# Six groups of two chunks in a chunked delta rule: chunk groups regrouped and w_in fetched earlier

## The chip, the cores and the metric

The kernel runs on one core of a Trainium2 chip. The metric is the device time of one execution in microseconds (us). The core has TensorE (PE in the profile, with its weight loads as PEld), VectorE (DVE), ScalarE (ACT), GpSimd (POOL) and SyncE (SP). Here SP issues every DMA, in program order.

## The reference

Two stages follow each other. The first is a delta-rule recurrence over 768 tokens, for 4 batch entries and 8 heads of 48 dimensions; k is divided by its norm:

```python
for t in range(S):
    kt, vt, bt = (k_n[:, :, t], v[:, :, t], beta[:, :, t, None])
    y[:, :, t] = np.einsum('bhd,bhde->bhe', q[:, :, t], state)
    v_old = np.einsum('bhde,bhd->bhe', state, kt)
    state = state + bt[:, :, :, None] * np.einsum('bhd,bhe->bhde', kt, vt - v_old)
```

The second takes the 3072 tokens' 384 values (8 heads of 48) through a wide layer of 1024:

```python
h = x @ w_in
e = np.exp(h - np.max(h, axis=-1, keepdims=True))
solu = h * e / (np.sum(e, axis=-1, keepdims=True) + 1e-09)
ln = (solu - mean(solu)) / np.sqrt(var(solu) + 1e-06) * g_ln
return ln @ w_out
```

## The kernel before

**Units.** The sequence is cut into 12 chunks of 64 tokens. A *unit* is one chunk of one pair of batch entries, so 128 rows; there are 24, u0 to u23, in the order chunk 0 pair 0, chunk 0 pair 1, chunk 1 pair 0 and so on. Names end in chunk and pair: `h_3_0` is h of u6, whose chunk is 3.

**Delta rule of a unit.** Inside a chunk the recurrence becomes a triangular system. `gram` multiplies K by K and K by Q per head on PE; ACT copies the first (`g`) to SBUF and SP sends it to DRAM (`gd`); DVE masks the second (`pm`). `chain` then applies the state: products `kps` and `yps`, r = v - kps on DVE, `ups` with the inverse, `u` on ACT, `cps` and the rest of `yps`, the state `st` updated on DVE, and the result split into two fp16 parts `xh` (ACT) and `xl` (DVE), which SP transposes by DMA (`xth`, `xtl`).

**Inversions of a group.** The triangular blocks of a *group* of chunks (the code's m) are inverted at once, one 32x32 block to a partition. `to_inv` gathers gd from DRAM into `ginv` (four DMAs with a full group); `norms` (DVE, first row `rst<-ginv`, last `nn`) makes norms and factors from its diagonal; `inv_begin` makes y with two DVE products, which a select on POOL makes triangular; `inv_step` runs 30 steps of two instructions each. For groups 0 and 1 a step's first ten columns are on DVE and the others on POOL; for later groups all is on POOL. `inv_end` copies the transpose on ACT (`ginv<-y`), sends y and the copy to DRAM (`zd`, `xd`) and gathers them back, laid out by unit (`zt`, `gx`, `gy`). `tlevel` joins the 32x32 blocks of a unit to 64x64 ones with small PE products (`mps`) and ACT copies into zt. The first of a group's chains needs this. Before, there are seven groups: chunk 0; chunks 1 and 2; 3 and 4; 5 and 6; 7 and 8; 9 and 10; chunk 11. In the groups of one chunk, half the partitions work on a copy of the other half.

**The wide layer of a unit.** `moe_h` makes h with 18 PE products of 512 columns (three fp16 passes over xl, xh and the two parts of w_in) in the one PSUM buffer for h; then the row maximum on DVE (`st<-h`, TENSOR_REDUCE), e on ACT, pr on DVE, the parts ph (ACT) and pl (DVE), two DMA transposes, and small row values, the rsqrt of them as a pow on POOL. `moe_out` has 24 PE products (`ops`), one DVE and one ACT instruction (`oc`) and the output DMA.

**Weights.** The weights come as 64-bit floats, whose bits `to_f32` reassembles: for each of 6 pieces of w_in a Square on ACT (`wc`), three DVE instructions and two POOL ones (`wf`), `win_hi` on ACT and `win_lo` on POOL; for each of 8 pieces of w_out the same with `wg`, `wout_hi` and, on DVE, `wout_lo`.

**What sets the order.** The kernel is recorded first. Each part is a stream with a time from a table at the end of the kernel function (in units of chunk steps; u0's chain is 0); that time is the priority of what it records. `Recorder.order` runs a list scheduler with a cost model over the record and so writes one fixed order for each engine, and there each instruction waits for all ahead of it. Every recorded instruction is issued from one line, L265, so the profile has one line for all, and the tile names tell them apart. The table puts a group's begin `tn` 5.4 steps before its end of preparation `e`, w_in's loads at -11.5 and -11.0 and group 1's gather at -10.8.

Of the kernel before, what the change touches and what calls it, by code (L numbers as in the profile page):

```python
# [8 lines left out]
F32 = mybir.dt.float32  # L9
# [10 lines left out]
NB = 7  # L20
# [280 lines left out]
def chunks_of(m):  # L301
    return [ch for ch in (2 * m - 1, 2 * m) if 0 <= ch < NC]
# [3 lines left out]
def kernel(  # L306
# [86 lines left out]
    def load_w_in(k, q, t0, t1):  # L393
        yield t0
        f = slice(512 * q, 512 * q + 512)
        raw = p3.tile([P, 512], w_in.dtype, tag="pr", name=f"wi_{k}_{q}")
        sp.dma_start(kb=512, out=raw, in_=w_in[k, q])
        yield t1
        w = p2.tile([P, 512], F32, tag="wf", name=f"wf_{k}_{q}")
        to_f32(w, raw, SC, 512, f"i{k}{q}")  # L400
        act.copy(out=win_hi[:, k, f], in_=w)
        gps.tensor_tensor(out=win_lo[:, k, f], in0=w, in1=win_hi[:, k, f], op=ALU.subtract)
# [95 lines left out]
    def gram(m, u, t0):  # L498
# [31 lines left out]
    last0 = [None]  # L530

    def to_inv(m):
        gi = p2.tile([P, 32, 32], F32, tag="ginv", name=f"ginv_{m}")
        ginv[m] = gi
        for b in range(4):
            blk = b % 2
            for z in range(1 if len(units(m)) == 4 else 2):
                src = gdt[m].rearrange("t u h j -> t (u h) j")
                n = H * len(units(m))
                ls = slice(0, n)  # L540
                sp.dma_start(
                    kb=128, out=gi[32 * b + 16 * z : 32 * b + 16 * z + n],
                    in_=src[32 * b : 32 * b + 32, ls, blk * 32 : blk * 32 + 32].rearrange("j l i -> l j i"),
                )
# [32 lines left out]
    def inv_end(m):  # L577
# [11 lines left out]
        n = 16 * len(chunks_of(m))  # L589
        src = gdt[m].rearrange("t u h j -> t (u h) j")  # L590
        for b in range(4):
            blk = b % 2
            r0 = 32 * b
            rows = slice(r0, r0 + 32)
            sp.dma_start(kb=128, out=zz[rows, 0:n, blk * 32 : blk * 32 + 32], in_=zd[r0 : r0 + n].rearrange("l j i -> j l i"))
            if blk == 0:
                for t, r1 in ((xx, r0), (xy, r0 + 32)):
                    sp.dma_start(kb=128, out=t[r1 : r1 + 32, 0:n], in_=xd[r0 : r0 + n].rearrange("l j i -> j l i"))
            else:
                sp.dma_start(kb=128, out=xx[rows, 0:n], in_=src[rows, 0:n, 0:32])  # L600
# [224 lines left out]
    for i in range(6):  # L825
        add(load_w_in(i // 2, i % 2, -11.5 if i < 2 else -11.0, -8 + 0.1 * i))
# [4 lines left out]

    for m in range(1, NB):
        f = 4 * m - 2
        nu = len(units(m))
        e = f if m > 1 else f - 2.5
        for u in range(nu):
            tg = e - 9 + 0.9 * u if m > 1 else -11.2 + 0.05 * u
            ch, bp = units(m)[u]
            add(once(tg - 0.9 if m > 1 else -11.8, lambda ch=ch, bp=bp: load_kq(ch, bp)))
            add(gram(m, u, tg))  # L840
            t = e - 1.9 + 0.9 * u
# [5 lines left out]
        add(inversion(m, tn + 0.6, e - 2.6 if m > 1 else -10))  # L847
# [35 lines left out]
def _lay(q, k, v, beta, moe_w_in, moe_w_out, moe_g_ln):  # L883
# [16 lines left out]
    bt = beta.reshape(2, 2, H, NC, 2, 32)  # L900
    bl = np.concatenate([bt[:, :, :, :1], bt, bt[:, :, :, -1:]], axis=3).reshape(2, 2, H, NB, 2, 2, 32)
# [27 lines left out]
```

## Time and profile before

| | before |
|---|---|
| time, median of 3 runs | 513.54 us (513.34 to 514.23) |
| time of the profiled execution | 512.04 us |
| its span | 510.2 us |
| busy PE / DVE / ACT / POOL | 368.2 / 318.6 / 192.9 / 294.0 us (72 / 62 / 38 / 58%) |
| DMA, mean of 16 engines | 70.8% for 72.21 MB |
| chain that ended last | POOL 28%, PE 22%, DVE 19%, issue 10%, DMA 9%, SP 7%, ACT 4% |

The page gives each engine's busy time, then the span in slices, then the chain of work that was followed back from the last instruction. The prediction also uses views of the trace. A row of a timeline has the start in us, the duration in us, the engine, the line, the operation, out<-in with shapes and, in brackets, the idle time ahead of it and what ended it. A row of the chain has start, duration, engine and out<-in; a group's row has the count, then busy us and mean ns. Rows of DMA issues have the count, KB each and us to landing.

### The profile page before, as it was taken

To read this page: it belongs to the slowest core of one execution; us is meant where nothing else is said; L and a number is where in the kernel's file an instruction comes from. 1 tells how busy PE (TensorE), PEld (TensorE's weight loads), DVE (VectorE), ACT (ScalarE), POOL (GpSimd) and SP (SyncE) were. 2 spreads that over 40 slices of the span, in tenths; PEclk is the share of its full clock that TensorE was granted. 3 is DMA by queue.
4 is the path that set the end of the run, shared out by engine and by line. 5 is a ranking of instruction groups with operands and counts; after the bars stand their busy time and mean duration, and the time that the engine had idled before them with its cause. 6 is when DMAs were issued, how large, how long until landed. Compare 5 with 4: busy or idle time off the path is not lost.

```text
span 510.2 us, 18246 instructions
## 1 busy us (share of the span) xinstructions
PE 368.2 (72%) x7744; PEld 233.9 (46%) x7744; DVE 318.6 (62%) x791; ACT 192.9 (38%) x382; POOL 294.0 (58%) x506
## 2 busy tenths in 40 slices
PE   3510070689579488997598997787969797899974
PEld 3410070455346345665366564444635464566532
DVE  3599999887884383655088664256597355455670
ACT  2210241465522143536144544224345345454450
POOL 3378385966558998984016886008989898100000
PEclk9999999877876699998799998898989899999998
DMA  8685662987989949977999587985656866744332
GB/s 212 159 255 98 155 169 65 161 171 174 172 162 165 179 113 160 168 135 161 189 165 144 145 162 151 160 162 95 107 118 144 145 114 128 131 64 99 73 68 61
DMA packets 180640, 72.21 MB, mean 142 GB/s; under 512 B 165520, under 2 KB 168976, under 8 KB 180560
## 3 DMA queue, kind: packets, MB, share of 16 engines
q1 hardware_dynamic: 180560, 71.06, 70.8%
q8 instruction: 60, 0.98, 0.9%
q14 instruction: 20, 0.16, 0.1%
HBM read 37.21 MB, written 16.52 MB: 105 GB/s over the span
## 4 chain that ended last, share of the span: by engine, by line
POOL 28%; PE 22%; DVE 19%; issue 10%; DMA 9%; SPq 7%; ACT 4%; POOLq 0%; DVEq 0%; ACTq 0%
POOL y L265 13%; POOL itmp L265 11%; PE h L265 7%; SPq L265 7%; PE ops L265 7%; DVE y L265 5%; DVE itmp L265 4%; DMA zt<-zd 3%; DMA ginv<-gd 3%; PE mps L265 2%; DVE wf L265 2%; DVE rst L265 1%; DVE st L265 1%; PE kps L265 1%; PE yps L265 1%
## 5 line engine op out<-in xcount | busy, mean ns | idle before, releaser
L265 POOL TENSOR_TENSOR y<-y,itmp 128x84 f32<-128x84 f32 (+16 forms) x190 | 100.7, 530 | 14.6
L265 POOL TENSOR_TENSOR itmp<-y,ginv 128x84 f32<-128x84 f32 (+16 forms) x190 | 93.3, 491 | 14.0
L265 DVE TENSOR_REDUCE st<-h 128x1 f32<-128x1024 f32 x24 | 29.3, 1222 | 87.5 <-PE h L265 82.2
L265 PE MATMUL qk<-kq 48*64 48x64 f32 x768 | 40.4, 269 | 24.9 <-DVE pm L265 15.6
L265 PE MATMUL gram<-kq 48*64 48x64 f32 x768 | 43.2, 270 | 18.8 <-DMA kq<-kq_dram 11.5
L265 POOL TENSOR_TENSOR st<-st,nhalf 128x1 f32<-128x1 f32 x24 | 13.2, 551 | 64.1 <-DVE st L265 64.1
L265 PEld LDWEIGHTS gram<-kq 48*64 48x64 f32 x768 | 37.5, 178 | 25.7 <-ACT g L265 6.3
L265 PEld LDWEIGHTS <-pth 128*128 128x128 f16 x384 | 37.6, 99 | 25.5 <-issue 1.7
L265 PE MATMUL h<-win_hi,xtl 128*128 128x512 f16 x144 | 45.4, 419 | 5.3 <-DVE pr L265 2.6
L265 PE MATMUL mps<-zt,gx 32*32 32x32 f32 x768 | 13.5, 205 | 48.6 <-issue 28.9
L265 PE MATMUL h<-win_lo,xth 128*128 128x512 f16 x144 | 46.7, 421 | 1.7 <-POOL win_lo L265 1.7
L265 PEld LDWEIGHTS qk<-kq 48*64 48x64 f32 x768 | 35.8, 178 | 25.3 <-DVE pm L265 16.1
L265 PEld LDWEIGHTS <-xth 128*128 128x128 f16 x288 | 28.4, 105 | 39.7 <-issue 14.8
L265 PE MATMUL ops<-wout_hi,ptl 128*128 128x384 f16 x192 | 38.7, 345 | 8.7 <-DMA ptl<-pl 6.8
L265 PE MATMUL h<-win_hi,xth 128*128 128x512 f16 x144 | 43.4, 411 | 0.0
L265 ACT ACTIVATE e<-h,st 128x1024 f32<-128x1024 f32 x24 | 26.7, 1114 | 38.0 <-DVE st L265 26.4
L265 POOL TENSOR_SCALAR_AFFINE_SELECT y<-y 128x1024 f32<-128x1024 f32 x7 | 9.4, 1346 | 53.5 <-DVE y L265 53.5
L265 DVE TENSOR_SCALAR st<-st 128x1 f32<-128x1 f32 (+1 forms) x216 | 35.5, 165 | 5.6
L265 PE MATMUL ops<-wout_lo,pth 128*128 128x384 f16 x192 | 36.9, 334 | 0.0
L265 PEld LDWEIGHTS mps<-zt,gx 32*32 32x32 f32 x768 | 10.1, 117 | 56.9 <-issue 34.8
L265 PE MATMUL ops<-wout_hi,pth 128*128 128x384 f16 x192 | 35.5, 326 | 0.0
L265 PE MATMUL cps<-u,kv 64*64 64x48 f32 x704 | 28.9, 235 | 9.1 <-ACT u L265 3.2
(94 smaller groups left out, 860.4 us busy)
## 6 DMA issues: line engine op xcount, KB each, us to landing
kq<-kq_dram SPq DMA_DIRECT2D x48, 192.0 KB, 4.5
kv<-kv_dram SPq DMA_DIRECT2D x24, 384.0 KB, 4.3
gd<-g SPq DMA_DIRECT2D x48, 128.0 KB, 3.3
out_dram<-oc SPq DMA_DIRECT2D x24, 192.0 KB, 2.2
zd<-y SPq DMA_DIRECT2D x7, 512.0 KB, 2.6
wi<-w_in_dram SPq DMA_DIRECT2D x6, 512.0 KB, 4.4
wo<-w_out_dram SPq DMA_DIRECT2D x8, 384.0 KB, 4.0
ginv<-gd SPq DMA_DIRECT2D x20, 128.0 KB, 4.2
```

Of the source, the lines that this page charges most:

```text
L265: fn(*[real(a) for a in args], **{k: real(a) for k, a in kw.items()})
```

## The change

There are six groups of two chunks each, so group m holds chunks 2m and 2m+1 and units 4m to 4m+3, and no group has copies. That moves all times of groups 2 and later by two steps (f = 4m), and group 2's begin lies 7 steps ahead, with its Gram products after u0's chain starts. Group 0 now has four units: four loads of kn for the norms, four Gram products, `tlevel` and `chain` with shifted priorities, and a shared tile (with tag "e") for g of its last two units. The gathers behind inversions 0 and 1 are cut in two halves of 16 blocks each. w_in's six pieces are loaded at -13.3, four of them into buffers of another pool (tag "kq"); the priority of their conversion stays at -8, so that it goes where the scheduler finds an engine idle. On the host, beta and kn are laid out for this.

```diff
-NB = 7
+NB = NC // 2
 def chunks_of(m):
-    return [ch for ch in (2 * m - 1, 2 * m) if 0 <= ch < NC]
+    return [2 * m, 2 * m + 1]
...
     def load_w_in(k, q, t0, t1):
-        raw = p3.tile([P, 512], w_in.dtype, tag="pr", name=f"wi_{k}_{q}")
+        raw = (p3 if k < 2 and q < 1 or k < 1 else p10).tile([P, 512], w_in.dtype, tag="pr" if k < 2 and q < 1 or k < 1 else "kq", name=f"wi_{k}_{q}")
...
     def load_kq(ch, bp):
-        if ch > 4:
+        if ch > 5:
             rec.after = raws[-1]
...
         act.activation(sq, k, AF.Square)
-        for v in (u, u + 2):
-            dve.tensor_reduce(out=xs[0][:, v], in_=sq, op=ALU.add, axis=AX.X)
+        dve.tensor_reduce(out=xs[0][:, u], in_=sq, op=ALU.add, axis=AX.X)
...
-        g = p2.tile([P, H, C], F32, tag="g", name=f"g_{ch}_{bp}")
+        if m or u < 2:
+            g = p2.tile([P, H, C], F32, tag="g", name=f"g_{ch}_{bp}")
+        else:
+            if u == 2:
+                ge[0] = p1.tile([P, 2, H, C], F32, tag="e", name="g_0")
+            g = ge[0][:, u - 2]
...
-        gps_ = ps_f.tile([P, H, C], F32, tag="fl", name=f"gram_{ch}_{bp}")
+        if m:
+            gps_ = ps_f.tile([P, H, C], F32, tag="fl", name=f"gram_{ch}_{bp}")
+        else:
+            gps_ = ps_ch.tile([P, H, C], F32, tag="ch", name=f"gram_{ch}_{bp}")
...
     def inv_end(m):
-        n = 16 * len(chunks_of(m))
-        for b in range(4):
-            sp.dma_start(kb=128, out=zz[rows, 0:n, blk * 32 : blk * 32 + 32], in_=zd[r0 : r0 + n].rearrange("l j i -> j l i"))
+        for l in (slice(0, 16), slice(16, 32)) if m < 2 else (slice(0, 32),):
+            n = l.stop - l.start
+            for b in range(4):
+                lanes = slice(r0 + l.start, r0 + l.stop)
+                sp.dma_start(kb=4 * n, out=zz[rows, l, blk * 32 : blk * 32 + 32], in_=zd[lanes].rearrange("l j i -> j l i"))
...
-    for bp in range(2):
-        add(once(-14 + .1 * bp, lambda bp=bp: load_kq(0, bp), lambda bp=bp: squares(bp)))
-        add(gram(0, bp, -13.5 + .01 * bp))
-        add(once(-9, lambda bp=bp: load_kv(0, bp), lambda bp=bp: fill_v(0, bp)))
-        add(tlevel(0, bp, -12.9 + 0.1 * bp, -12.85 + 0.1 * bp))
+    for u, (ch, bp) in enumerate(units(0)):
+        add(once(-14 + .1 * u, lambda ch=ch, bp=bp: load_kq(ch, bp)))
+        add(once(-13.7 + .01 * u, lambda u=u: squares(u)))
+        add(gram(0, u, -13.5 + .01 * u))
+        add(once(-9 + u, lambda ch=ch, bp=bp: load_kv(ch, bp)))
+        add(once(-9 + u, lambda u=u: fill_v(0, u)))
+        add(tlevel(0, u, -5 + u, -4.95 + u), -8)
...
-        add(load_w_in(i // 2, i % 2, -11.5 if i < 2 else -11.0, -8 + 0.1 * i))
+        add(load_w_in(i // 2, i % 2, -13.3 + 0.01 * i, -8 + 0.1 * i))
...
-        f = 4 * m - 2
-        e = f if m > 1 else f - 2.5
+        f = 4 * m
...
+            if m == 2:
+                tg = -2 + 0.9 * u
...
-        tn = e - 5.4 if m > 1 else -10.8
+        tn = f - 5.4 if m > 2 else f - 7 if m > 1 else -10.8
...
-        add(chain(m, u, i, i + 0.13, i + 0.25), -CH)
+        add(chain(m, u, i, i + 0.13, i + 0.25), -CH if m else -14)
```

Three places show how the written order moves. In its rows, numbers behind a name's chunk and pair are a buffer's; the shape is that of the output, and x2 or x4 says how many like it follow each other. The first is SP's queue around the gather of group 1 (`ginv_1<-gd_1`). Before:

```order
L265 DMA gd_1_390<-g_2_1_475 64x512 x2
L265 DMA kv_0_0_517<-kv_dram 128x768
L265 DMA kv_0_1_533<-kv_dram 128x768
L265 DMA ginv_1_553<-gd_1_390 32x32x32 x4
L265 DMA gx_1_586<-gd_1_390 32x32x32 x2
L265 DMA g_sb_602<-g_ln_dram 128x8
L265 DMA kq_3_0_604<-kq_dram 48x1024 x2
L265 DMA zd_0_623<-y_0_388 128x1024
```

After:

```order
L265 DMA zt_0_214<-zd_0_604 32x16x32
L265 DMA gd_1_541<-g_3_0_700 64x512 x2
L265 DMA gd_1_541<-g_3_1_755 64x512 x2
L265 DMA kv_1_0_829<-kv_dram 128x768
L265 DMA kv_1_1_886<-kv_dram 128x768
L265 DMA_TRANSPOSE xth_0_0_912<-xh_0_0_905 128x3x128
L265 DMA ginv_1_916<-gd_1_541 32x32x32
L265 DMA_TRANSPOSE xtl_0_0_953<-xl_0_0_910 128x3x128
L265 DMA ginv_1_916<-gd_1_541 32x32x32 x3
```

The gather of group 1 stood ahead of group 0's way back through DRAM (`zd_0`); it now stands behind that way back, behind two kv loads and among u0's two transposes.

The second is DVE around the row maximum of u0, `st_0_0<-h_0_0`. Before:

```order
L265 TENSOR_SCALAR wg_0_1182<-wo_0_960 128x384
L265 SCALAR_TENSOR_TENSOR wg_0_1182<-wo_0_960,wg_0_1182 128x384 x2
L265 TENSOR_SCALAR wg_1_1237<-wo_1_1021 128x384
L265 SCALAR_TENSOR_TENSOR wg_1_1237<-wo_1_1021,wg_1_1237 128x384 x2
L265 TENSOR_REDUCE st_0_0_1267<-h_0_0_1152 128x1
```

After:

```order
L265 TENSOR_TENSOR itmp_1_30_0_1605<-y_1_1179,ginv_1_916 128x10
L265 TENSOR_TENSOR y_1_1179<-y_1_1179,itmp_1_30_0_1605 128x10
L265 TENSOR_TENSOR pm_4_1_1608<-qk_4_1_1269,mask_93 128x512
L265 TENSOR_REDUCE st_0_0_1614<-h_0_0_996 128x1
L265 TENSOR_SCALAR st_0_0_1614<-st_0_0_1614 128x1
L265 SCALAR_TENSOR_TENSOR st_0_0_1614<-st_0_0_1614 128x1
L265 TENSOR_SCALAR st_0_0_1614<-st_0_0_1614 128x1 x4
L265 TENSOR_SCALAR wg_0_1661<-wo_0_1177 128x384
```

The row maximum of u0 stood behind two pieces of w_out; it now stands behind the last step of inversion 1, and w_out's first piece behind it.

The third is PE inside h of u6 (`h_3_0`) after the change, with group 2's first block products (`mps`, the second product of u8's blocks in the lower rows):

```order
L265 MATMUL mps0_2_0_3162<-zt_0_214,gx_2_2390 32x32 x16
L265 LDWEIGHTS xth_3_0_2777
L265 MATMUL h_3_0_3141<-win_lo_351,xth_3_0_2777 128x512
...
L265 MATMUL mps0_2_0_3162<-msb_2_0_3182,gx_2_2390 32x32 x2
L265 MATMUL mps32_2_0_3189<-msb_2_0_3182,gy_2_3065 32x32 x2
...
L265 MATMUL h_3_0_3141<-win_hi_344,xth_3_0_2777 128x512
```

In program order they stand apart only by weight loads and repeated rows of the same kind; h of u6 is thus finished behind these products, which need zt of group 2. On DVE the norms of group 3 stand behind u6's pr:

```order
L265 TENSOR_REDUCE st_3_0_3214<-h_3_0_3141 128x1
L265 TENSOR_SCALAR st_3_0_3214<-st_3_0_3214 128x1
L265 SCALAR_TENSOR_TENSOR st_3_0_3214<-st_3_0_3214 128x1
L265 TENSOR_SCALAR st_3_0_3214<-st_3_0_3214 128x1 x4
L265 SCALAR_TENSOR_TENSOR pr_3_0_3291,st_3_0_3214<-h_3_0_3141,e_3_0_3260 128x1024
L265 TENSOR_SCALAR rst_3_3336<-ginv_3_2954 128x32
```

Before the change, the norms of groups 3, 4, 5 and 6 stood behind the row maxima of u2, u7, u12 and u13.

More of the change, by code (lines that the diff above doesn't have):

```diff
@@ L529 @@
     ginv, yt = {}, {}
-    last0 = [None]
+    last0, ge = [None], [None]
     def to_inv(m):
@@ L534, in to_inv @@
         ginv[m] = gi
+        src = gdt[m].rearrange("t u h j -> t (u h) j")
         for b in range(4):
             blk = b % 2
[L537 to L544, printed above, removed]
+            r = slice(32 * b, 32 * b + 32)
+            sp.dma_start(kb=128, out=gi[r], in_=src[r, :, blk * 32 : blk * 32 + 32].rearrange("j l i -> l j i"))
     def inv_begin(m):
@@ L588, in inv_end @@
         xy = p1.tile([P, 4 * H, 32], F32, tag="gy", name=f"gy_{m}")
-        n = 16 * len(chunks_of(m))
         src = gdt[m].rearrange("t u h j -> t (u h) j")
-        for b in range(4):
-            blk = b % 2
-            r0 = 32 * b
-            rows = slice(r0, r0 + 32)
-            sp.dma_start(kb=128, out=zz[rows, 0:n, blk * 32 : blk * 32 + 32], in_=zd[r0 : r0 + n].rearrange("l j i -> j l i"))
[L596 to L600, printed above, removed]
+        for l in (slice(0, 16), slice(16, 32)) if m < 2 else (slice(0, 32),):
+            n = l.stop - l.start
+            for b in range(4):
+                blk = b % 2
+                r0 = 32 * b
+                rows = slice(r0, r0 + 32)
+                lanes = slice(r0 + l.start, r0 + l.stop)
+                sp.dma_start(kb=4 * n, out=zz[rows, l, blk * 32 : blk * 32 + 32], in_=zd[lanes].rearrange("l j i -> j l i"))
+                if blk == 0:
+                    for t, r1 in ((xx, r0), (xy, r0 + 32)):
+                        sp.dma_start(kb=4 * n, out=t[r1 : r1 + 32, l], in_=xd[lanes].rearrange("l j i -> j l i"))
+                else:
+                    sp.dma_start(kb=4 * n, out=xx[rows, l], in_=src[rows, l, 0:32])
         ztx[m], gxt[m] = zz, (xx, xy)
@@ L832 @@
     for m in range(1, NB):
-        f = 4 * m - 2
-        nu = len(units(m))
-        e = f if m > 1 else f - 2.5
-        for u in range(nu):
-            tg = e - 9 + 0.9 * u if m > 1 else -11.2 + 0.05 * u
-            ch, bp = units(m)[u]
+        f = 4 * m
+        for u, (ch, bp) in enumerate(units(m)):
+            tg = f - 9 + 0.9 * u if m > 1 else -11.2 + 0.05 * u
+            if m == 2:
+                tg = -2 + 0.9 * u
             add(once(tg - 0.9 if m > 1 else -11.8, lambda ch=ch, bp=bp: load_kq(ch, bp)))
             add(gram(m, u, tg))
-            t = e - 1.9 + 0.9 * u
+            t = f - 1.9 + 0.9 * u
             add(tlevel(m, u, t, t + 0.4))
@@ L844 @@
             add(once(f + u - 0.9, lambda m=m, u=u: fill_v(m, u)))
-        tn = e - 5.4 if m > 1 else -10.8
+        tn = f - 5.4 if m > 2 else f - 7 if m > 1 else -10.8
         add(begin(m, tn, tn + (0.5 if m > 1 else 0.01)))
-        add(inversion(m, tn + 0.6, e - 2.6 if m > 1 else -10))
+        add(inversion(m, tn + 0.6, f - 2.6 if m > 1 else -10))
     order = [(m, u) for m in range(NB) for u in range(len(units(m)))]
@@ L898, in _lay @@
     kq = con(np.stack([tr(k), tr(q)], axis=5))
-    bt = beta.reshape(2, 2, H, NC, 2, 32)
-    bl = np.concatenate([bt[:, :, :, :1], bt, bt[:, :, :, -1:]], axis=3).reshape(2, 2, H, NB, 2, 2, 32)
+    bl = beta.reshape(2, 2, H, NB, 2, 2, 32)
     bl = con(bl.transpose(1, 5, 4, 0, 2, 3, 6).reshape(P, NB, 32))
@@ L909, in _lay @@
     return {
-        "kn_dram": con(kn[0]),
+        "kn_dram": con(kn[:2].reshape(4, P, H, D)),
         "kv_dram": kv,
```

## The prediction

> **What bounds the kernel now.** I read the chain that ended last first, then the windows by stage, then the places where a unit's h is finished, then the rows of the chain between two inversions. A unit is one chunk of 64 tokens for one pair of batch entries; u0 to u23 are worked on in this order.
>
> ```profile
> POOL 28%; PE 22%; DVE 19%; issue 10%; DMA 9%; SPq 7%; ACT 4%; POOLq 0%; DVEq 0%; ACTq 0%
> ```
>
> No engine owns the chain. It goes over POOL while an inversion runs, and over DMA, SP, PE and DVE between two of them.
>
> ```profile
> core 0: us, PE busy (x) PEld busy (x) DVE busy (x) ACT busy (x) POOL busy (x), PEclk, DMA share, GB/s
> 108.00:204.00 96.00, 71.85 (x1601) 46.05 (x1595) 63.66 (x150) 38.12 (x79) 71.13 (x109) 0.80 0.88 165
> 204.00:448.00 244.00, 207.13 (x4567) 129.03 (x4565) 137.21 (x353) 105.28 (x214) 149.94 (x269) 0.94 0.76 143
> ```
>
> PE is at 85% in the long middle stage, so little is left there for a change that only removes idle time. In the stage ahead of it DVE, POOL and DMA are all at 66 to 88%, and no engine explains 96 us by itself.
>
> ```profile
> 107.96 1.22 DVE L265 TENSOR_REDUCE st<-h 128x1 f32<-128x1024 f32 x1 [0.39 <-PE h L265]
> 156.25 1.64 DVE L265 SCALAR_TENSOR_TENSOR pl<-pr,st,ph 128x1024 f16<-128x1024 f32 x1 [0.37 <-ACT ph L265]
> 204.19 1.22 DVE L265 TENSOR_REDUCE st<-h 128x1 f32<-128x1024 f32 x1 [5.41 <-PE h L265]
> 334.65 1.22 DVE L265 TENSOR_REDUCE st<-h 128x1 f32<-128x1024 f32 x1 [6.36 <-PE h L265]
> 430.44 1.22 DVE L265 TENSOR_REDUCE st<-h 128x1 f32<-128x1024 f32 x1 [4.42 <-PE h L265]
> 448.39 1.22 DVE L265 TENSOR_REDUCE st<-h 128x1 f32<-128x1024 f32 x1 [7.62 <-PE h L265]
> 490.42 1.23 DVE L265 TENSOR_REDUCE st<-h 128x1 f32<-128x1024 f32 x1 [1.89 <-PE h L265]
> ```
>
> The DVE timeline: each reduction is the row maximum that follows a finished h; here those of u0, u4, u12, u18, u19 and u23, and u2's pl. I call them R0, R4 and so on. From R0 to R4 a unit takes 24 us, from R4 to R23 15.1 us, from R18 to R23, with the last inversion over, 12.0 us. R23 to the end of the span is 19.8 us.
>
> ```profile
> 144.45 1.26 POOL L265 TENSOR_SCALAR_AFFINE_SELECT y<-y 128x1024 f32<-128x1024 f32 x1 [8.20 <-DVE y L265]
> 189.43 1.26 POOL L265 TENSOR_SCALAR_AFFINE_SELECT y<-y 128x1024 f32<-128x1024 f32 x1
> 270.88 1.26 POOL L265 TENSOR_SCALAR_AFFINE_SELECT y<-y 128x1024 f32<-128x1024 f32 x1 [4.95 <-DVE y L265]
> 344.46 1.26 POOL L265 TENSOR_SCALAR_AFFINE_SELECT y<-y 128x1024 f32<-128x1024 f32 x1 [29.61 <-DVE y L265]
> 389.93 1.26 POOL L265 TENSOR_SCALAR_AFFINE_SELECT y<-y 128x1024 f32<-128x1024 f32 x1
> 188.11 1.99 ACT L265 COPY ginv<-y 128x1024 f32<-128x1024 f32 x1
> 310.97 1.99 ACT L265 COPY ginv<-y 128x1024 f32<-128x1024 f32 x1 [6.59 <-POOL y L265]
> 431.36 1.96 ACT L265 COPY ginv<-y 128x1024 f32<-128x1024 f32 x1
> ```
>
> The POOL and ACT timelines: the select starts the POOL inversion of groups 2 to 6 (call the starts A2 to A6), the ACT copy behind it marks its end (E). Three of them give A to E: 43.7, 40.1 and 41.4 us; I take **41**. POOL then waits up to 29.6 us for the next group's y. So POOL isn't full: inversions alternate with a return path.
>
> ```profile
> 312.98 1.97 DMA xd<-ginv
> 320.36 4.27 DMA zt<-zd
> 324.67 0.45 PE mps L265 x30
> 337.76 0.19 DVE L265 TENSOR_SCALAR rst<-ginv 128x32 int32<-128x32 int32 x1 [1.69 <-DMA ginv<-gd]
> 341.90 1.23 DVE L265 TENSOR_TENSOR ginv<-ginv,nn 128x1024 f32<-128x1024 f32 x1
> ```
>
> The chain and DVE around it: E4 at 310.97, xd and the gathers into zt, group 4's first block product at 324.67 (13.7 after E4), the rest of u12's h, R12 at 334.65, group 5's norms from 337.76 (DVE has them behind R12), its two 1.23 us products, A5 at 344.46. The return path took 33.5 us.
>
> **The change part by part.** It takes one POOL inversion away (five become four) and gives group 0 four units instead of two. What is priced is when A2 comes and how long the ring of inversions and return paths runs from there.
>
> *The front.*
>
> ```profile
> 3.11 5.07 DMA kn<-kn_dram
> 25.06 1.47 DVE ginv L265
> 36.75 3.17 SPq L265 DMA_DIRECT2D ginv<-gd  x4
> 53.06 1.94 ACT L265 COPY ginv<-y 128x1024 f32<-128x1024 f32 x1 [19.80 <-issue]
> 57.54 1.22 DVE L265 TENSOR_TENSOR ginv<-ginv,nn 128x1024 f32<-128x1024 f32 x1
> 60.10 2.01 DVE wf L265 x2
> 72.30 0.49 ACT L265 ACTIVATE xh<-yps 128x384 f16<-128x384 f32 x1 [2.15 <-PE yps L265]
> 87.92 2.00 ACT L265 COPY ginv<-y 128x1024 f32<-128x1024 f32 x1 [11.74 <-DVE y L265]
> ```
>
> Now inversion 0 begins at 25.06 and ends at 53.06, u0's xh comes at 72.30, and inversion 1, whose gather was issued at 36.75, runs right behind inversion 0, 57.54 to 87.92. In the change the fourth kn is issued behind the first gd, and ACT copies the fourth g after its square: with the 5.07 us of a kn landing I add 2 us (0 if it lands unnoticed, 5 if all waits), and 1 us for w_in conversion ahead of the first step: inversion 0 ends near 56. The gathers into zt are now twice as many and stand behind one more gd, so for xh I take the 19.2 us of now plus 1.5: near 76.5. Only then can SP issue group 1's gather, since it stands behind u0's xth and xtl; now it stands ahead of everything of u0. Two transposes and four pieces at 0.8 us end near 82, and it lands near 86:
>
> ```profile
> gd<-g SPq DMA_DIRECT2D x48, 128.0 KB, 3.3
> ginv<-gd SPq DMA_DIRECT2D x20, 128.0 KB, 4.2
> zt<-zd SPq DMA_DIRECT2D x20, 128.0 KB, 4.2
> zt<-zd SPq DMA_DIRECT2D x8, 64.0 KB, 2.9
> L265 DVE SCALAR_TENSOR_TENSOR xl<-yps,xh 128x384 f16<-128x384 f32 x24 | 13.2, 549 | 0.1
> ```
>
> Norms are 4.1 us (337.76 to 341.90), the inversion 30.4 us as now, less the w_in pieces in it (the 2.01 us row and as much again), plus five chain instructions of about 0.55 us that DVE has between its steps. The order puts u0's reduction behind the last step, so **R0 is near 120**, 12 us later than now, though its h needs only xtl and w_in, ready by then. Bounds: 114 if the gather lands at 80, 126 if every piece waits as at its worst. The w_in conversions save nothing here: they end earlier, and R0 doesn't wait for them.
>
> The Trainium skill (DMA: Bandwidth & Descriptors, Rules for kernel authors) would have small transfers coalesced, since under 64 KB they are mostly overhead; here groups 0 and 1 are cut into halves. The rows say 2.9 us for a 64 KB piece against 4.2 for 128 KB, so a half does land sooner. By the rule alone the half would gain nothing and the sum would be 1.3 us higher.
>
> *R0 to A2.*
>
> ```profile
> L265 DVE SCALAR_TENSOR_TENSOR wg<-wo,wg 128x384 int32<-128x384 int32 x16 | 11.0, 689 | 0.4
> L265 DVE TENSOR_SCALAR wg<-wo 128x384 int32<-128x384 int32 x8 | 5.7, 715 | 1.8 <-DMA gd<-g 1.3 <-POOL win_lo L265 0.5
> L265 DVE TENSOR_TENSOR wout_lo<-wg,wout_hi 128x384 f16<-128x384 f32 x8 | 4.5, 575 | 3.5 <-ACT wout_hi L265 3.4
> ```
>
> Group 2's norms now stand ahead of u2's row maximum; in the change behind u2's pl. From R0 to the end of u2's pl it takes 49.9 us now. Less the norms and two products in it (6.6), plus two w_out slices that DVE has done before R0 now and does after it in the change (2 x (0.715 + 2 x 0.689), and one wout_lo, 0.575: 4.8), it is 48: norms near 168, and 6.6 us later **A2 near 174.7**, 30 us later than now. Bounds: 40 us if the stalls in that stretch go, 55 if the gather is late.
>
> *The ring.* Four inversions of 41 us are 164. Three return paths: PE's order has 15 of u6's 18 h products ahead of group 2's second block product, and DVE has group 3's norms behind u6's pr; groups 4 and 5 stand the same way behind R10 and R14. So E to block product 13.7, some 3 us of h and copies, 1.2 for the maximum, up to 4 for pr, 4.1 and 2.5 for norms and products: 28, 27 and 29 (group 5's gather stands behind four transposes of u13). Together 84; from below 75 with no wait for a gather, from above 3 x 33.5 = 100.5 as measured. E5 is then near 174.7 + 164 + 84 = 422.7. From E6 to R19 it is 17.0 us now; the change has u18's output product between group 5's block product and u19's h, so up to 24: I take 20, **R19 near 442.7**, against 448.39. Behind it the same units, 61.8 us to the end: 504.5. Lies beside other work: the smaller number of gathers, norms and POOL steps, and kv's scaling. The profiled run took 512.04 with a span of 510.2; the median is 513.54, 3.3 over the span. Forecast: **507.8, said as 508 us.**
>
> **The rivals.** *The cover rival, faster:* PE isn't held by the ring at all, because its block products come when zt is there. For it: DVE works only 63.66 of the 96 us from R0 to R4, and w_out is done on POOL ahead of A2, where now two slices are caught inside inversion 2. R4 at 190, 19 units at 14.5 us (between 12.0 and 15.1), 19.8 us: 485, a time of 488. Against it: the ring holds u5's exp behind E2 in ACT's order. *The late-ring rival, slower:* mechanism as forecast, but A2 comes at 177, every return path costs the measured 33.5, and R19 stands 24 behind E5: 177 + 164 + 100.5 + 24 + 61.8 = 527, a time of 531. With R19 24 behind E5 it loses to the kernel before from E5 later than about 424 (448.39 less 24). Rows speak for it: 33.5 is the one path measured whole. *It doesn't do what it says:* w_in early is of no use, and the inversion removed is one that lay beside other work; then R19 stays near 448.39 and the time at the median, 513.5.
>
> **How the numbers follow.** The forecast's ring (498 to 515) 0.42, the cover rival 0.22, the late ring 0.28, no effect 0.08. A measurement of this kernel tells 0.2%, about 1 us, from no change. Faster: 0.22 and 0.30 of the forecast's 0.42. Same: 0.04 of it, 0.04 of the last. Slower: 0.28, 0.08 and 0.04. So 0.52, 0.08, 0.40. The forecast's own range is 498 to 515; with both rivals, leaving a tenth out on each side, 484 to 528.
>
> **What would show it.** R0 near 120 with inversion 1's last DVE step right ahead of it; group 1's gather issued behind u0's transposes after 76; w_out done on POOL before A2 near 175; exactly four selects behind that, 67 to 72 us apart; PE waiting for zt inside u6's and u10's h; R19 some 20 us behind the last ACT ginv copy. It is wrong if selects follow each other closer than 60 us, if R0 comes before 108, or if PE waits for something else at the group borders.

## The result and the profile after

The changed kernel took 529.79 us in the median of 4 runs (528.26 to 532.73), the kernel before 513.44 us (512.15 to 514.23). The ratio is 1.0328, with a 95% interval of 1.0277 to 1.0378. It is slower, where 508 was forecast, and it lies outside the range, 1.8 us above its upper end. The profiled execution took 529.23 us, with a span of 527.5 us. Some kernels below had executions more than 1.5% over their fastest; the ratios leave these out, the medians do not.

First the page's busy line of the changed kernel, then its windows by stage, cut at the row maxima of u0 (R0), u4 (R4) and u19 (R19):

```profile
PE 382.6 (73%) x7744; PEld 243.9 (46%) x7744; DVE 306.7 (58%) x771; ACT 192.0 (36%) x382; POOL 258.6 (49%) x445
```

```profile
core 0: us, PE busy (x) PEld busy (x) DVE busy (x) ACT busy (x) POOL busy (x), PEclk, DMA share, GB/s
0.00:125.80 125.80, 54.12 (x1492) 43.47 (x1492) 84.79 (x204) 28.75 (x61) 73.10 (x123) 0.90 0.68 159
125.80:197.60 71.80, 59.99 (x1099) 36.16 (x1102) 53.81 (x129) 34.20 (x70) 39.92 (x52) 0.79 0.79 161
197.60:465.40 267.80, 217.53 (x4542) 135.22 (x4538) 135.59 (x354) 103.90 (x207) 141.83 (x261) 0.89 0.69 132
465.40:527.50 62.10, 50.94 (x632) 29.04 (x629) 32.52 (x87) 25.15 (x45) 3.72 (x10) 0.95 0.35 72
```

POOL lost 35 us of work and the kernel became slower. R0 came 17.8 us later than before (125.8 against 108.0), but R4 came 6.6 us earlier (197.6 against 204.2): what the front loses up to u0 it has regained by u4. The loss is all in the third row. From R4 to R19 the change took 267.8 us, the kernel before 244.2 (448.39 less 204.19): 23.6 more for the same fifteen units. The last stage is the same, 62.1 against 61.8.

That row also shows of what the 23.6 consist. PE is busy 217.5 us in it against 207.1 in nearly the same stretch before, with about as many products (4542 against 4567), at a granted clock of 0.89 against 0.94. So 10 us are the same work at a lower clock (0.89 x 217.5 and 0.94 x 207.1 are 194 and 195). The other 13 are time without work on PE (50.3 us against 36.9).

The POOL and ACT timelines of the changed kernel, put together in order of time, with the four selects that start the POOL inversions (A2 to A5) and the ACT copies that mark their ends (E2 to E5):

```profile
177.57 1.27 POOL L265 TENSOR_SCALAR_AFFINE_SELECT y<-y 128x1024 f32<-128x1024 f32 x1 [13.51 <-DVE y L265]
217.34 1.98 ACT L265 COPY ginv<-y 128x1024 f32<-128x1024 f32 x1 [3.16 <-POOL y L265]
247.36 2.25 POOL L265 TENSOR_SCALAR_AFFINE_SELECT y<-y 128x1024 f32<-128x1024 f32 x1 [21.62 <-DVE y L265]
287.46 1.96 ACT L265 COPY ginv<-y 128x1024 f32<-128x1024 f32 x1 [6.62 <-POOL y L265]
316.76 1.27 POOL L265 TENSOR_SCALAR_AFFINE_SELECT y<-y 128x1024 f32<-128x1024 f32 x1 [19.05 <-DVE st L265]
356.26 1.96 ACT L265 COPY ginv<-y 128x1024 f32<-128x1024 f32 x1 [4.81 <-POOL y L265]
391.92 1.27 POOL L265 TENSOR_SCALAR_AFFINE_SELECT y<-y 128x1024 f32<-128x1024 f32 x1 [14.64 <-DVE y L265]
433.52 1.99 ACT L265 COPY ginv<-y 128x1024 f32<-128x1024 f32 x1 [2.47 <-POOL y L265]
```

The inversions took 39.8, 40.1, 39.5 and 41.6 us, together 161.0. Between them lie three full return paths of 30.0, 29.3 and 35.7 us, together 95.0. From A2 to the last E it is 256.0 us, in the kernel before 286.9 (144.45 to 431.36, with five inversions). So the change did shorten this stretch, by 31 us: the inversions took 161.0 us in place of 207.5, but the three return paths 95.0 in place of 79.4 for four. Two of the four borders of the kernel before were nearly free: its A3 stood 1.3 us behind an E (189.43 against 188.11), since those norms were done early, and its A6 4.2 us (389.93 against 385.78). The other two took 40.4 (230.46 to 270.88) and 33.5 us. The two E of the kernel before that the prediction does not show (ACT timeline):

```profile
230.46 1.95 ACT L265 COPY ginv<-y 128x1024 f32<-128x1024 f32 x1 [5.71 <-POOL y L265]
385.78 1.97 ACT L265 COPY ginv<-y 128x1024 f32<-128x1024 f32 x1 [6.21 <-POOL y L265]
```

The 31 us were more than spent elsewhere: A2 came 33.1 us later, and from the last E to R19 it took 31.9 us against 17.0. That leaves R19 17.0 us later than before.

The last piece in detail. PE's timeline around the return of group 5, and six of the windows of 2 us there (columns as above):

```profile
438.80 0.23 PE L265 MATMUL yps<-st,kq 48*64 48x48 f32 x1 [2.92 <-DVE xl L265]
444.31 0.31 PE L265 MATMUL mps<-zt,gx 32*32 32x32 f32 x2 [2.31 <-DMA zt<-zd]
448.29 0.64 PE L265 MATMUL mps<-zt,gx 32*32 32x32 f32 x30 [3.67 <-DMA zt<-zd]
```

```profile
438.00:440.00 2.00, 1.20 (x62) 1.23 (x62) 0.56 (x2) 0.57 (x2) 0.00 (x0) 0.89 1.02 174
440.00:442.00 2.00, 2.00 (x9) 0.45 (x6) 0.55 (x1) 0.00 (x0) 0.00 (x0) 0.50 1.32 153
444.00:446.00 2.00, 0.31 (x2) 0.18 (x2) 1.43 (x3) 0.84 (x2) 0.00 (x0) 0.50 1.17 160
450.00:452.00 2.00, 2.00 (x7) 0.93 (x8) 0.72 (x2) 1.30 (x6) 1.12 (x3) 0.50 0.58 158
452.00:454.00 2.00, 2.00 (x41) 1.01 (x40) 0.00 (x0) 0.00 (x0) 0.33 (x2) 0.70 1.00 193
454.00:456.00 2.00, 2.00 (x72) 1.52 (x70) 0.00 (x0) 1.14 (x4) 0.00 (x0) 1.00 0.12 23
```

zt lands 14.8 us behind the last E, about as forecast (13.7). But then it takes 17.1 us to R19: in PE's order u17's output product, three units' block products and u20's and u21's first products stand ahead of u19's h, and for nearly the first 5 us of this the granted clock is 0.50. It had fallen behind the wait that ended at 438.80, and as PE went on waiting it did not rise until work came almost without a break. In the kernel before, only three of u19's h products were left when zt landed, and R19 came 1.2 us after that wait, with the clock at 1.00 from E6 on:

```profile
447.16 0.45 PE L265 MATMUL mps<-zt,gx 32*32 32x32 f32 x30 [2.40 <-DMA zt<-zd]
```

### The profile page after: what moved, and what is told of

Its sections match the earlier page's. It is cut to its first block, busy times and chain, and to the rows that moved or that the text cites. A ratio compares the mean times of both kernels' runs of the same rounds, so it can differ in the third digit from the quotient of the medians.

```text
span 527.5 us, 18160 instructions
## 1 busy us (share of the span) xinstructions
PE 382.6 (73%) x7744; PEld 243.9 (46%) x7744; DVE 306.7 (58%) x771; ACT 192.0 (36%) x382; POOL 258.6 (49%) x445
## 4 chain that ended last, share of the span: by engine, by line
POOL 30%; issue 19%; PE 15%; DVE 14%; SPq 9%; DMA 9%; ACT 4%; POOLq 0%; DVEq 0%; ACTq 0%
POOL y L265 13%; POOL itmp L265 12%; SPq L265 9%; PE h L265 5%; DVE y L265 4%; PE ops L265 4%; DVE itmp L265 4%; DMA kq<-kq_dram 3%; DMA zt<-zd 2%; POOL st L265 2%; PE ups L265 1%; PE mps L265 1%; DVE st L265 1%; DMA kn<-kn_dram 1%; DVE wg L265 1%
## 5 line engine op out<-in xcount | busy, mean ns | idle before, releaser
L265 POOL TENSOR_TENSOR y<-y,itmp 128x84 f32<-128x84 f32 (+16 forms) x160 | 80.0, 500 | 12.3
L265 POOL TENSOR_TENSOR itmp<-y,ginv 128x84 f32<-128x84 f32 (+16 forms) x160 | 76.6, 479 | 12.1
L265 DVE TENSOR_REDUCE st<-h 128x1 f32<-128x1024 f32 x24 | 29.3, 1223 | 88.4 <-PE h L265 79.6
L265 PE MATMUL gram<-kq 48*64 48x64 f32 x768 | 43.0, 270 | 34.1 <-DMA kq<-kq_dram 24.6
L265 PE MATMUL ops<-wout_hi,ptl 128*128 128x384 f16 x192 | 41.5, 364 | 7.4 <-DMA ptl<-pl 7.0
L265 PE MATMUL h<-win_hi,xth 128*128 128x512 f16 x144 | 45.2, 423 | 0.0
L265 PE MATMUL ups<-r,zt 64*64 64x48 f32 x704 | 29.4, 241 | 13.0 <-DVE r L265 13.0
L265 PE MATMUL ops<-wout_lo,pth 128*128 128x384 f16 x192 | 38.1, 342 | 0.0
L265 PE MATMUL yps<-st,kq 48*64 48x48 f32 x704 | 29.7, 240 | 11.3 <-DVE xl L265 10.5
L265 DVE SCALAR_TENSOR_TENSOR pl<-pr,st,ph 128x1024 f16<-128x1024 f32 x24 | 33.4, 1391 | 7.2 <-ACT ph L265 4.2
L265 ACT ACTIVATE ph<-pr,st 128x1024 f16<-128x1024 f32 x24 | 27.6, 1149 | 27.3 <-DVE pr L265 24.8
```

What stands on the lines that cost most here:

```text
L265: fn(*[real(a) for a in args], **{k: real(a) for k, a in kw.items()})
```

## The experiments

Each edit starts from the changed kernel unless it says otherwise; what isn't shown is unchanged. Ratios are to the kernel before, which ran on the same chip. It took 513.4 to 515.0 us on the chips used, so a difference between two times of the table can be off by 1.5 us; ratios are the safer comparison. From R4 to R19 the kernel before took 244.2 us.

| run | time, us | ratio (95% interval) | R4 to R19 in its profile, us |
|---|---|---|---|
| the change | 529.8 | 1.0328 (1.0277 to 1.0378) | 267.8 |
| short_inv | 510.3 | 0.9921 (0.9893 to 0.9949) | 249.0 |
| before_short | 500.4 | 0.9736 (0.9698 to 0.9773) | 233.3 |
| norms_1_earlier | 521.2 | 1.0128 (1.0103 to 1.0153) | 256.0 |
| norms_2_earlier | 517.1 | 1.0035 (1.0002 to 1.0067) | 245.5 |
| norms2_short | 496.4 | 0.9671 (0.9623 to 0.9720) | 225.5 |
| less_pe | 507.2 | 0.9877 (0.9844 to 0.9911) | 240.0 |
| w_in_late | 526.5 | 1.0223 (1.0181 to 1.0266) | 268.6 |
| before_w_in_early | 538.8 | 1.0502 (1.0454 to 1.0549) | 258.8 |
| gather_first | 530.1 | 1.0294 (1.0260 to 1.0328) | 266.2 |
| front_both | 517.8 | 1.0077 (1.0045 to 1.0109) | 257.4 |
| group2_early | 539.2 | 1.0467 (1.0427 to 1.0508) | 263.4 |
| kv_ahead | 521.9 | 1.0136 (1.0109 to 1.0163) | 259.1 |
| kv_only | 528.6 | 1.0278 (1.0233 to 1.0323) | 265.6 |
| keep_clock | 527.8 | 1.0232 (1.0174 to 1.0289) | |
| three_together | 516.1 | 0.9995 (0.9967 to 1.0023) | 243.2 |
| front_and_kv | 519.9 | 1.0089 (1.0056 to 1.0121) | 256.7 |
| front_kv_norms1 | 519.2 | 1.0077 (1.0044 to 1.0110) | 271.4 |
| norms2_kv_late_w_in | 509.9 | 0.9927 (0.9899 to 0.9954) | 241.9 |

### Is it the inversions?

**short_inv.**

```diff
+    def left_out(kw):
+        t = kw.get("in1")
+        for v in (kw.get("out"), t):
+            n = v.root.name.split("_") if isinstance(v, View) else [""]
+            if n[0] == "itmp" and int(n[1]) > 1 and 13 <= int(n[2]) <= 18:
+                return True
+        return False
...
     for o in ops:
         for fn, args, kw in o.calls:
+            if left_out(kw):
+                continue
```

> The changed kernel with steps 13 to 18 of the four POOL inversions (groups 2 to 5) left out, the order of everything else word for word the same; so its output is not the reference's. In the changed kernel's trace these six steps take POOL 8.5 us of each inversion. Ring theory (from A2 on, inversions and return paths alternate and every unit waits for them): the whole 4 x 8.5 = 34 us comes off, a time of 496 (up to 505 if PE takes over in places), and the return paths stay at 27 to 34 us. PE theory (the middle is slow because PE is at its limit under a lower clock, 0.89 against 0.94): POOL's work is hidden, at most 5 us come off, 525 to 530.

19.5 us came off, between the two. In its trace the inversions are together 27.1 us shorter (31.3, 31.6, 33.3 and 37.7), and the return paths 8.0 us longer (34.2, 33.3 and 35.5). Its window from R4 to R19:

```profile
200.50:449.50 249.00, 212.25 (x4546) 133.37 (x4546) 134.21 (x355) 103.87 (x207) 110.77 (x213) 0.88 0.73 142
```

So the inversions are on the path, but a return path is no fixed price. I read it so that it holds the units that stand between an E and the next norms, and these have a pace of their own: a shorter inversion leaves more of them to the return.

**before_short.** The same edit on the kernel before.

> The kernel before with steps 13 to 18 of its five POOL inversions (groups 2 to 6) left out, order unchanged; its output is not the reference's. This tests the premise that the kernel before is held by its inversions too: 5 x 8.5 = 42 us of POOL's work are gone. If inversions and return paths set the pace before as well, 20 us or more come off (493 or less). If the 16.3 us that a unit takes there from R4 to R19 are set by something else (PE's work and the waits inside a unit's own chain), 0 to 8 us come off: 506 to 514.

13.9 us of some 42 came off, a third, against 57% in the changed kernel (19.5 of 34). The premise of the forecast, that alternation sets the pace before as it does after, is only a third true. By this an inversion that is removed there is worth less than its length; no run removes a whole one.

**norms_1_earlier and norms_2_earlier.** With d = 1 and d = 2:

```diff
-            tg = f - 9 + 0.9 * u if m > 1 else -11.2 + 0.05 * u
+            tg = f - (9 + d) + 0.9 * u if m > 1 else -11.2 + 0.05 * u
...
-        tn = f - 5.4 if m > 2 else f - 7 if m > 1 else -10.8
+        tn = f - (5.4 + d) if m > 2 else f - 7 if m > 1 else -10.8
```

> The changed kernel with the Gram products and the norms of groups 3 to 5 put one step earlier in the table: the norms of group 3 stand behind u4's pr instead of u6's, those of group 4 behind u8's pl instead of u10's maximum, those of group 5 behind u13's maximum instead of u14's. Ring theory: the next inversion no longer waits for the group's own return path, so POOL starts it right behind the one before; A2 stays at 177, A3 follows E2 within 10 us instead of 28, and R19 comes 30 to 50 us before 465: 480 to 500. PE theory: selects come earlier, but PE is full; 525 to 530.

> The same, two steps earlier: norms of group 3 ahead of u4's maximum, of group 4 behind u8's pr, of group 5 behind u12's maximum. Ring theory: as one step earlier, with the return path gone from all three places, 475 to 495. PE theory: 525 to 530. A loss against one step earlier would mean that Gram products put earlier hold the units that are due.

8.6 and 12.7 us came off: the direction of the ring theory, far from its size. norms_2_earlier alone brings the kernel within 0.4% of the one before. In norms_2_earlier A3 comes at 220.97, ahead of E2 at 224.88 (POOL and ACT timelines):

```profile
220.97 1.27 POOL L265 TENSOR_SCALAR_AFFINE_SELECT y<-y 128x1024 f32<-128x1024 f32 x1
224.88 1.99 ACT L265 COPY ginv<-y 128x1024 f32<-128x1024 f32 x1 [0.60 <-POOL y L265]
292.07 2.25 POOL L265 TENSOR_SCALAR_AFFINE_SELECT y<-y 128x1024 f32<-128x1024 f32 x1 [17.43 <-DVE y L265]
360.78 1.27 POOL L265 TENSOR_SCALAR_AFFINE_SELECT y<-y 128x1024 f32<-128x1024 f32 x1 [18.49 <-DVE st L265]
```

One return path is gone, but A4 and A5 still follow 71 and 69 us behind, with POOL idle ahead of them: their norms now stand behind u8's pr and u12's maximum, and on the way to these PE waits for zt (3.3 us until 238.8, 6.2 until 295.3). Nor did all that the ring gained reach the units. The three return paths are 42.3 us shorter in sum and the last E comes 31.4 us earlier (402.15 against 433.52), but R4 comes 12.3 us later (209.9), and from the last E to R19 it takes 53.3 us instead of 31.9, so R19 comes only 10.0 us earlier. So once the norms are early, R19 no longer follows from the last E alone.

**norms2_short and less_pe.** Both take norms_2_earlier further: one with the six steps left out, the other with one pass of h left out of all units:

```diff
+    def left_out(kw):
+        v, r = kw.get("out"), kw.get("rhs")
+        return isinstance(v, View) and v.root.name.startswith("h_") and isinstance(r, View) and r.root.name == "win_lo"
...
+            if left_out(kw):
+                continue
```

> The changed kernel with norms two steps earlier (517.1) and steps 13 to 18 of the four POOL inversions left out (8.5 us each); its output is not the reference's. Neither PE's work (less by a third of h: 507.2) nor the inversions of the kernel before (13.9 of 42 us came off) account for the 16.4 us a unit takes there. If inversions still hold it, half or more of the 34 us come off: 500 or less. If the latency of a unit's own way (h, maximum, e, pr, transposes, with the POOL powers and PE's waits inside) holds it, at most 8: 509 to 517.

> The changed kernel with norms two steps earlier (measured 517.1) and, of h's three passes, the second (xh by w_in's low part, 6 of 18 products) left out, order unchanged otherwise; its output is not the reference's. In the changed kernel's trace these 144 products take PE 46.4 us, 1.9 us per unit. If PE is what is left once the return path is relaxed, all of it comes off: 15 x 1.9 = 29 us from R4 to R19 and some more at both ends, 475 to 487. If inversions still hold the units, under 12 us: 505 to 517.

20.8 us of 34 came off with the shorter inversions, 9.9 us with a third of h gone. So with the norms early the inversions still count for more (61% of their saving passes through) than PE's amount of work. The windows from R4 to R19, less_pe's first and norms2_short's behind it:

```profile
204.40:444.40 240.00, 197.95 (x4285) 127.43 (x4280) 128.75 (x335) 102.88 (x205) 137.93 (x256) 0.86 0.75 139
```

```profile
205.40:430.90 225.50, 200.59 (x4348) 126.22 (x4350) 127.80 (x334) 103.13 (x205) 105.45 (x204) 0.94 0.78 148
```

less_pe lacks a third of h's products, and PE is busy nearly as long as in norms2_short, 198.0 against 200.6 us, at a clock of 0.86 against 0.94. It also has 42.1 us without work there against 24.9. In these two runs PE works faster where it waits less. So part of what less_pe left out came back as a lower clock, and its 9.9 us are not a clean price of PE's work.

### The front

**w_in_late and before_w_in_early** exchange the fetch of w_in between the two kernels:

```diff
-        raw = (p3 if k < 2 and q < 1 or k < 1 else p10).tile([P, 512], w_in.dtype, tag="pr" if k < 2 and q < 1 or k < 1 else "kq", name=f"wi_{k}_{q}")
+        raw = p3.tile([P, 512], w_in.dtype, tag="pr", name=f"wi_{k}_{q}")
...
-        add(load_w_in(i // 2, i % 2, -13.3 + 0.01 * i, -8 + 0.1 * i))
+        add(load_w_in(i // 2, i % 2, -11.5 if i < 2 else -11.0, -8 + 0.1 * i))
```

> The changed kernel with w_in's six pieces fetched at the times and into the buffers of the kernel before. Theory that w_in's early fetch is what delayed group 1 (its four kq loads stand behind all of w_in on SP, and so its Gram products, its stores and its gather): the norms of group 1 come 8 to 12 us before 87.8, R0 near 115 instead of 125.8, and since everything behind follows, a time near 519. Rival: the gather of group 1 is held by u0's transposes whenever w_in comes; R0 stays within 3 us of 125.8 and the time within 3 us of 530.

> The kernel before, seven groups, with only w_in fetched as in the change. In six groups the early fetch cost 3.3 us. If it is harmful because it stands ahead of the next groups' loads on SP: 514 to 520 here too. If it helps where group 0 is small and the first h waits for w_in (in the kernel before PE waits 2.31 us for win_hi ahead of u0's h): 505 to 512, and this is the version that beats both.

w_in_late is 3.3 us faster than the change, and its R0 comes 3.2 us earlier: the early fetch costs a little and gains nothing, and the grouping alone is still 2.2% slower than the kernel before. In the kernel before, the early fetch costs 24.6 us, but by another way than either expectation had: the new times gave another written order, in which PE has the column sums of w_out ahead of u1's h and waits there for w_out to be converted. R1 comes 49.5 us later than in the kernel before (178.0 against 128.5) and A2 26.6 us later (171.0 against 144.5).

```profile
119.12 0.48 PE L265 MATMUL cs<-wout_lo,ones 128*128 128x384 f16 x1 [19.99 <-DVE wout_lo L265]
```

**gather_first.** Group 1's loads, Gram products and gather ahead by priority:

```diff
-            add(once(tg - 0.9 if m > 1 else -11.8, lambda ch=ch, bp=bp: load_kq(ch, bp)))
-            add(gram(m, u, tg))
+            add(once(tg - 0.9 if m > 1 else -11.8, lambda ch=ch, bp=bp: load_kq(ch, bp)), -1.75 if m == 1 else 0)
+            add(gram(m, u, tg), -2.15 if m == 1 else 0)
...
-        add(begin(m, tn, tn + (0.5 if m > 1 else 0.01)))
+        add(begin(m, tn, tn + (0.5 if m > 1 else 0.01)), -3.3 if m == 1 else 0)
```

> The changed kernel with the kq loads, Gram products and gather of group 1 put ahead by priority, so that the gather stands ahead of group 0's way back through DRAM again, as in the kernel before; w_in still early. Theory that the place of this gather made the front late: inversion 1 runs right behind inversion 0 and ends near 96 instead of 127.3, R0 comes near 108 to 112, A2 near 165 instead of 177.6, and as the ring starts earlier the whole of it comes off: a time of 514 to 519. Rival: DVE and POOL are full up to A2 anyway (inversions and weight conversions only change places); R0 moves, A2 stays within 4 us of 177.6 and the time within 4 us of 530.

Inversion 1 ended 24 us earlier and the time did not change. The ACT copy and the first row maximum of this run:

```profile
101.54 2.01 ACT L265 COPY ginv<-y 128x1024 f32<-128x1024 f32 x1 [4.02 <-DVE y L265]
129.15 1.22 DVE L265 TENSOR_REDUCE st<-h 128x1 f32<-128x1024 f32 x1 [0.96 <-PE h L265]
```

R0 now waits for h itself. The forecast had R0 at the right time, behind the last step of inversion 1, but that was not its only hold: ahead of it PE waited 7.3 us for the loads of group 2's Gram products (kq, until 124.90).

**front_both** also delays group 2's loads and Gram products (`2.5 if m == 2` in the first two shifts).

> Group 1's gather first as measured (530.1, R0 still at 129), and now also group 2's loads and Gram products put later, out of u0's h. Theory that two holds lay side by side ahead of R0 (inversion 1 on DVE, and group 2's Gram products, which wait for their loads, inside u0's h on PE): with both gone R0 falls to 105 to 118. What the time does then depends on group 2, whose gather is later: 515 to 535. If R0 stays within 4 us of 126, it is the work ahead of it (weights on DVE and POOL) that sets it.

R0 came at 118.7, so group 2's Gram products were part of the second hold. R4 stayed at 197.1, and yet the time fell by 12 us. The gain came from further on: in this run's written order the norms of group 3 had moved from behind u6's pr to ahead of u5's, and A3 follows E2 by 6.0 us (225.22 to 231.19) instead of 30.0.

**group2_early.** Loads, Gram products and `begin` of group 2 with a shift of -4.

> The changed kernel with the loads, Gram products, gather and norms of group 2 put four steps ahead by priority: its norms stand right behind u2's row maximum, among the last w_out pieces, instead of behind u2's pl. Ring theory: the POOL inversions end 255.9 us behind their start at A2, 31 us less than in the kernel before, and lose 33 us by starting at 177.6 instead of 144.5; so if A2 comes 15 to 25 us earlier (153 to 163), E5 and R19 come at least half of that earlier and the time is 508 to 521. If the units' own pace behind R4 sets it, E5 follows the units and the time stays within 4 us of 530.

A2 came 13.8 us earlier, at 163.8, and the run is 9.4 us slower than the change. The last w_out pieces now stand inside inversion 2, which took 49 us instead of 40, and R4 came 14 us later. So this order bought an earlier A2 with what it overtook, which is needed too; no other order was tried.

### kv's scaling and the clock

In the changed kernel POOL scales kv of u11 and u15 behind a whole inversion, and DVE's r waits for it:

```profile
DVE r L265 <- POOL kv L265: 14.0, 2, 8.7
```

**kv_ahead** gives `fill_v` a shift of -2 from group 2 on; **kv_only** moves just these two POOL instructions ahead of step 16 of the inversion.

> The changed kernel with POOL's scaling of kv two steps earlier in priority from group 2 on: u11's and u15's scaling stand inside or ahead of the inversions that they stood behind. In the changed kernel's trace r of u11 and of u15 wait 8.67 and 5.34 us for them, and PE 4.67 and 4.95 us for r. Theory that these waits lie on the ring: 6 to 12 us come off, 518 to 524. Rival: they lie beside it, since the next step waits for the inversion's end and its return path anyway: 528 to 531.

> kv_ahead gave 8 us, but there the norms of group 4 had also moved, from behind u10's maximum to ahead of it. Here nothing moves but two POOL instructions, the scaling of u11's and u15's kv, from behind inversions 3 and 4 to ahead of their step 16. If the late scaling is itself the wait (r of these units waited 14.0 us in two places): 520 to 525. If kv_ahead's gain came from the moved norms alone: 527 to 531.

kv_ahead is 7.9 us faster, kv_only 1.2 us, which these runs can't tell from nothing. In kv_only the two waits are gone and R9 comes 6.0 us earlier (282.7 against 288.7), but R10 only 1.7 us: there the units wait for the inversion's return all the same. I take the gain of kv_ahead to be that of the norms of group 4, which had moved along with the order: its A4 follows E3 by 15.8 us (290.79 to 306.54) instead of 29.3. The forecast's nothing for kv's scaling holds.

**keep_clock.** Added products where PE waits for zt:

```diff
         with rec.atomic():
+            if u == 0 and nm not in ("0_0", "1_0"):
+                for i in range(24):
+                    pe.matmul(ns=0, out=tiles[0].rearrange("p a n i -> p (a n i)"), lhsT=ones, rhs=wout_hi[:, 0, 0:256], start=True, stop=True)
```

> The changed kernel with 24 added products of 256 columns (at full clock some 2.6 us, by the 0.33 us that three 384-column ones overlap to: results not used) ahead of each of the four first block products of groups 2 to 5, where PE waits for zt; nothing else moves. In the changed kernel the granted clock falls to 0.50 for some 3 to 13 us behind such waits. If it falls because PE idles there, the granted clock from R4 to R19 rises from 0.89 to 0.92 or more and the time falls by 2 to 8 us (522 to 528); if it falls for another reason, the clock stays and the added products cost 0 to 10 us (530 to 540).

Undecided: single runs lie between 523.6 and 532.5 us, and the interval of its ratio touches that of the change.

### Sums

> Group 1's gather first, norms two steps earlier and kv's scaling two steps earlier, all at once. If the ring theory holds and the three gains add (13 from norms as measured, 12 from the gather, 6 from kv): 495 to 503, below both kernels. If PE with its low clock sets the rest, at most half of that: 510 to 516.

> Group 1's gather first, group 2's Gram products out of u0's h, and kv's scaling two steps earlier. If front_both's gain (12 us) and kv_ahead's (8 us) lie at different places of the ring they add: 508 to 512, a little below the kernel before. If front_both only gained because the norms of group 3 came to stand one unit earlier, and kv's scaling waits on that same path: 514 to 519.

> As front_and_kv with the Gram products of group 2 a step less late, and the norms of groups 3 to 5 one step earlier as well. If the ring is what is left, the 9 us that norms one step earlier gave come off too: 498 to 507, below both kernels. If a unit takes 16 us whatever the inversions do, R19 comes 15 x 16.2 = 243 us behind R4 and the time is 510 to 516.

> Six groups with the norms two steps earlier, kv's scaling two steps earlier and w_in fetched as in the kernel before: what each gave singly is 13, up to 8 and 3 us. If they add, 506 to 512 and below the kernel before (514); if the ring's waits are one and the same, as front_and_kv and three_together had it, 512 to 517.

three_together has gather_first, norms_2_earlier and kv_ahead; front_and_kv has front_both and kv_ahead; front_kv_norms1 has front_both with 1.5 in place of 2.5, kv_ahead and norms_1_earlier. None is below the kernel before, and front_and_kv is no faster than front_both alone. I read it so that the single gains were mostly one wait, taken away twice; no run shows that by itself. norms2_kv_late_w_in has norms_2_earlier, kv_ahead and w_in_late, and at 509.9 us it is below both kernels, by 0.7% against the kernel before.

## Why the prediction was wrong

By its own steps, with what was forecast and what the profile of the change has:

| step | forecast | measured |
|---|---|---|
| u0's xh | 76.5 | 77.0 |
| norms of group 1 | 86 | 87.8 |
| R0 | 120 (114 to 126) | 125.8 |
| A2 | 174.7 | 177.6 |
| four inversions | 164 | 161.0 |
| three return paths | 84 (75 to 100.5) | 95.0 |
| last E to R19 | 20 (up to 24) | 31.9 |
| R19 | 442.7 | 465.4 |
| R19 to the end of the span | 61.8 | 62.1 |

The step that failed is the sum behind A2: two of its terms were priced too low, the return paths by 11.0 us and the stretch from the last E to R19 by 11.9. Together these are 22.9 us, and R19 missed by 22.7; A2, 2.9 us late, and the inversions, 3.0 us short, cancel.

- **The front** was right in its sum (A2 2.9 us off) and half right in its reason. That A2 fitted is partly luck: R0 came 5.8 us later than forecast, and from R0 to A2 it took 51.8 us where the sum had 54.7. R0 did stand behind the last step of inversion 1, but gather_first and front_both show a second hold beside it, h of u0 with group 2's Gram products in it, and neither moved the end by way of R0. The side remark that early w_in saves nothing held; it costs some 3 us.
- **The return paths** are the first term that was mis-sized, 84 for 95.0. The third is the furthest off, 35.7 for 29: group 5's norms waited for their gather, which I had priced at 2 us for its place behind u13's transposes, and u14's h was finished 7.3 us behind its block product (370.05 to 377.32), where the sum had 3.

```profile
385.23 0.19 DVE L265 TENSOR_SCALAR rst<-ginv 128x32 int32<-128x32 int32 x1 [5.22 <-DMA ginv<-gd]
```

- **The last E to R19** is the second mis-sized term, 20 for 31.9. I had taken the kernel before's 17.0 plus a product. In that kernel the last inversion belongs to u22 and u23, which come later than R19; in the change it belongs to u20 to u23, and their block products and first chain products stand in PE's order ahead of u19's h. I had the place from the order and sized it by one output product; PE was at work for 16.8 of the 17.1 us there, some of it at half clock.
- **PE's clock** had no term. From R4 to R19 it made some 10 us of the 23.6; they are not a further term of the sum, since they lie within the stretches of the table.
- **The premise** that the ring is what the kernel before pays for was too strong. before_short lets a third of a shorter inversion through. The change took away one inversion that was worth less than its length there, and put a full return path at each of three borders where the kernel before had two of four almost free.
- **The late-ring rival** (chance 0.28) comes nearest to what happened: its R19 of 465.5 (177 + 164 + 100.5 + 24) against 465.4 and its time of 531 against 529.8. That its R19 fits to 0.1 us is luck: it had the returns 5.5 us and the inversions 3.0 too long and the last stretch 7.9 too short. The 33.5 us were not the one return path measured whole either, as the prediction says: from 230.46 to 270.88 the kernel before has another, of 40.4 us. In sum the whole path was nearer than the parts (100.5 and 84 for 95.0), border by border it was not: the first two took 30.0 and 29.3 us, for which the parts gave 28 and 27. The cover rival fell: R4 came at 197.6 and not 190, and units took 17.9 us, not 14.5.

That R4 is 6.6 us earlier while R0 is 17.8 us later can be read in the traces, though no run tests it. In the kernel before POOL did the last w_out piece at 170.87, inside inversion 2, and PE waited 5.59 us for its column sums (until 175.78); PE also waited 1.92 us inside u4's h for zt of group 2 (until 201.59). In the change the last w_out piece stands at 162.25, ahead of A2, and inversion 2 ends only behind R4.

What stays open: how much of the low clock is cause and how much effect, as keep_clock did not decide it, and what sets the units' pace once the norms are early.

## What to carry to other kernels

When an engine alternates between a long job and a way back through others, look at each border for itself before counting jobs: a border with its preparation done early can be nearly free (1.3 us here), and a change that takes one job away can make every border cost its full price. Price such a way back from both sides: here the sum of its parts, with hardly a wait in it, came out below the measured total and the one whole path that was used above it. Look for every whole one that the trace has, and price the way from the last job to the end as carefully. After an edit to a schedule's table, compare the whole written order and not only the part that was meant: two of the runs here (kv_ahead and front_both) gained by something that had only moved along.

## What the runs showed of the hardware

A wait on PE was paid for twice. The granted clock fell to 0.50 behind a wait of 2.92 us (until 438.80) and stayed there over two more, of 2.31 and 3.67 us, as the windows from 438 to 456 us show, and came back to 1.00 only when work had come almost without a break for nearly 5 us (from 448.3 to between 452 and 454). The Trainium skill (TensorE: Matmul & The Clock Gate, Part 1) gives an idle and a busy window of about 3.4 us for this. The trace agrees in kind, but here a wait below that length was enough, and the way back was somewhat longer. Over a whole kernel it shows as busy time: PE's 7744 products took 368.2 us before and 382.6 us in the change, at mean granted clocks of 0.920 and 0.884 (either product of the two is 338 to 339 us), so a busy PE is no measure of its work.
